# Fused attention, soft mixture of experts and gated FFN: the heads in another order, a load later, the weight conversion two steps ahead, and the copies of a step behind the next silu

## The chip, the core and the metric

The kernel runs on one core of one Trainium2 chip. The metric is the device time of one execution in microseconds (us). The core's engines are TensorE (PE, with its weight loads as PEld), VectorE (DVE), ScalarE (ACT), GpSimd (POOL) and SyncE (SP); 16 DMA engines move data between HBM and the on-chip memory. Each engine takes its instructions in the order in which the program gives them to it, and waits on semaphores for the others.

## The reference

Three stages follow each other; everything is float32 except the FFN weights, which arrive as float64.

```python
# q, k, v: 4 batches x 8 heads x 576 x 64
scores = q @ k.T / 8                      # heads 0..3: local mask, 0 <= i-j < 32
                                          # heads 4..7: strided mask, i >= j and i%32 == j%32
x = softmax(mask(scores)) @ v             # heads side by side: x is 2304 x 512

logits = x @ phi                          # 32 slots = 8 experts x 4
d = softmax(logits over the 2304 tokens)
slot = d.T @ x                            # 32 x 512
slot_out[e] = relu(slot[e] @ w1[e]) @ w2[e]       # w1: 8 x 512 x 1024, w2: 8 x 1024 x 512
x = softmax(logits over the 32 slots) @ slot_out  # c @ slot_out, 2304 x 512

g = x @ w_gate                            # 512 x 1536
out = (g * sigmoid(g) * (x @ w_val)) @ w_out      # 1536 x 512, out is 2304 x 512
```

## The kernel before

**Attention (0 to 117 us).** A unit is one head of two batches (a batch pair); there are 16, in the order of `HORDER`, each in three steps t of three blocks of 64 query rows. The tokens of the strided heads are laid out so that their mask is a narrow band too, which makes both kinds of head the same work with widths 96 and 80. The loop takes two steps at a time, n and n+1: the score matmuls (`qk`, L296) of both, DVE's mask and maximum (L302), ACT's exponential (L314), the transposes of the step two before (`tr`, L321) with ACT's copy of them (L324), the product with v of the step four before (`pv`, L334), and DVE's normalisation. Behind the second head of each pair of heads the rows are transposed (`xtr`, L360) and multiplied with phi (`logits`, L380, 8 matmuls; a strided pair writes its tokens back in the plain order). Once all four pairs of heads of a batch pair have added to one bank of PSUM, `tok_max` and the token softmax follow.

**Loads.** SP issues the loads in program order: q, k and v of a unit some units ahead (L267, L268, L274), and between them halves of 1 MB weight tiles (`load_half`, L178). These go into 14 buffers called `w`, into the three shared tiles `s1`, `s0`, `s2`, which also hold q, k, v and the local mask `ml`, and into attention's own tiles. Eight semaphores are used in turn for the loads, so that each load waits until the one eight before it has landed. `WORDER` gives the order in which the weights take the 14 buffers; a later load into the same buffer waits for the last reader of the earlier one.

**Mixture of experts (117 to 153 us).** 16 weight tiles w1 (`w1_mm`, L656) and 16 tiles w2 (L745) are used as they land. Between the matmuls of w2, `c_soft` makes the softmax over the slots (two halves) and eight `c_tr` turn it (3 transposes each, L716, and a DVE copy, L719) into `cs`; the table `CTR` tells after which w2 tile.

**FFN (153 to 360 us).** Since x = c @ slot_out, the kernel first multiplies the weights by slot_out. For each of 12 column tiles f, `a_mm` (L805) makes soT x w, ACT copies it (`asb`, L808), `a_st` (L812) spreads it and ACT and DVE split it into `St` (L813, L814). The FFN then runs over a list of steps (a range of f by five token blocks): `gv` (two matmuls, L825 and L826), silu on ACT (`sg`, L831), the product on DVE (`h`, L832), its high part on ACT (`hh`, L833) and the rest of it on POOL (`hl`, L834). `omm` (12 matmuls, L852) of a step runs `LAG` = 3 steps behind it. `h` has two buffers, so that h of a step waits for hl of the step two before; hh and hl have four. The partial sums go to `acc` by ACT or DVE (L875) or are added to it by DVE (L878), and the last range writes `out` (L880, L861).

**Weight conversion.** The float64 weights arrive as pairs of words. Tiles g (gate and value of one f) and o (two rows of f of the last matrix) are converted in halves: ACT takes the magnitude (L227, the first half of `prep`), POOL clamps it (L228), and DVE does three parts, `shift`, `low`, `sign` (L232, L236, L240), in the order of `ORDER`. `stage` starts a half on ACT and POOL, `part` runs one DVE part; at most two halves are staged, and parts are run in a step as far as its room goes. `force` does what is missing at once when a step needs a tile that isn't ready: all instructions that stand before it, `a_mm` and `a_st` too. `HEAD` is the order at the entry of the FFN: a = a_mm, s = a_st, g = stage, w = a warm matmul, p = parts. `load_g` (L686) loads the FFN's weights into four `g` tiles, which are laid over the memory of the `w` tiles and the first of which waits for whatever last used it.

Of the kernel before, what the change touches and what calls it, by code (L numbers as in the profile page):

```python
# [17 lines left out]
S = 576  # L18
# [6 lines left out]
HORDER = (0, 1, 4, 5, 2, 3, 6, 7)  # L25
# [7 lines left out]
WORDER = list(range(1, 13)) + list(W2ORDER[:2])  # L33
# [5 lines left out]
LAG = 3  # L39
WT = (0, 0)  # L40
# [3 lines left out]
CTR = {9: 1, 10: 1, 11: 1, 12: 1, 13: 1}  # L44
CTE = (1,)
SLOT0 = [(4, [(0, 0, 9)]), (6, [(1, 0, 5)]), (8, [(1, 5, 9)])]
STG = 1
# [8 lines left out]
HEAD = "a0 a1 g s0 w1 s1 p1 w1"  # L56
# [55 lines left out]
def build(ctx: ExitStack, tc: tile.TileContext, cst, phi, qh, kh, vh, w1, w2, wgv, wo, out):  # L112
# [34 lines left out]
    ml, ms = s1[:, VW + K:VW + K + 192], s3[:, VW + S:VW + S + 720]  # L147
# [158 lines left out]
    def expo(u, t):  # L306
        W = WID[UNITS[u][1] // 4]
        sm, mx = sc.pop((u, t))
        o = 288 * ((3 * u + t) % 2)
        e = tmp[:, o:288 + o].rearrange("p (j k) -> p j k", j=3)  # L310
        if W < 96 and u % 4 == 2 and t < 2:
            DVE.memset(e[:, :, 0:96 - W], 0.0)
        for j in range(3):
            ACT.activation(out=e[:, j, 96 - W:96], in_=sm[:, j, 0:W], func=AF.Exp, scale=-1.0, bias=mx[:, j:j + 1])  # L314
        ex[u, t] = e
# [50 lines left out]
    def logits(bp, y, st):  # L366
        first, last = (y, st) == (0, 0), (y, st) == (1, 1)
        if first:
            lg[bp] = bank("lg", 1)
        a = xT.pop((bp, y, st))  # L370
        for hf in range(2):
# [145 lines left out]
    with tc.manual_schedule():  # L517
# [16 lines left out]
        load_half(2)  # L534
# [40 lines left out]
        for bp in range(2):  # L575
            for y in range(2):
                for st in range(2):
                    u = 8 * bp + 4 * st + 2 * y + 1
# [134 lines left out]
        def c_tr(bp, b, hf):  # L713
            ps = bank("tr", 2)
# [6 lines left out]
        ctr = [(c_tr, (bp, b, hf)) for bp in range(2) for b in range(2) for hf in range(2)]  # L721
# [20 lines left out]
        for n, j in enumerate(W2ORDER):  # L742
# [7 lines left out]
            if n < 2:  # L750
                c_soft(n)
# [3 lines left out]
            for _ in range(CTR.get(n, 0)):  # L755
                fn, a = ctr.pop(0)
                fn(*a)
# [63 lines left out]
        def gv(bi, f):  # L821
# [11 lines left out]
            ACT.copy(hh[bi, f][:, 0:n], h[:, 0:n])  # L833
            POOL.tensor_tensor(out=hl[bi, f][:, 0:n], in0=h[:, 0:n], in1=hh[bi, f][:, 0:n].bitcast(F32),  # L834
                               op=ALU.subtract)
# [4 lines left out]
        def omm(p, bi, f):  # L840
# [6 lines left out]
            def mm(t, terms):  # L847
                z = len(ob[t])
                c = 512 // z
                for k, o in enumerate(ob[t]):  # L850
# [4 lines left out]
                    if last and 2 in terms:  # L855
                        if end:
# [4 lines left out]
                            SP.dma_start(out=out[r:r + 128, c * k:c * k + c], in_=tmp[:, 0:c])  # L861
# [70 lines left out]
        split_hi(0)  # L932
        split_lo(0, 0)
        split_lo(0, 1)
        for step in HEAD.split():
# [5 lines left out]
            elif k == "g":  # L941
                stage(-2)
            elif k == "p":
# [4 lines left out]
        for n in range(len(seq) + LAG):  # L948
# [17 lines left out]
            if n < len(seq):  # L966
                force(n, ("g", seq[n][2]))
                gv(*seq[n][1:])
            while staged and staged[0][0] <= n and PART <= room:
                room -= PART  # L970
                part(n)
            if n >= STG:
                stage(n)
                if n < 2 * STG:
                    stage(n)
# [20 lines left out]
```

## Time and profile before

| What | Value |
|---|---|
| Time, median of 3 runs (lowest to highest) | 361.76 us (359.48 to 364.25) |
| Profiled execution: its time, its span | 362.2 us, 360.4 us |
| Mean granted TensorE clock | 0.994 |
| PE busy | 338.7 us, 94% |
| PEld busy | 243.9 us, 68% |
| DVE busy | 219.4 us, 61% |
| ACT busy | 186.8 us, 52% |
| POOL busy | 132.6 us, 37% |
| DMA moved | 71.94 MB, mean 200 GB/s |

The profile is of one execution on the hardware. Busy times overlap between engines; a share over the whole span is a mean over stages with different limits. The span of the profiled execution starts at its first instruction, and its time is 1.8 us longer than that.

### The profile page before, as it was taken

Reading aid. Unit: us, or ns where it says so; the run is one execution under the profiler, and the core shown is the slowest. Engines: PE = TensorE matmul, PEld = TensorE weight load, DVE = VectorE, ACT = ScalarE, POOL = GpSimd, SP = SyncE. Lnnn points to the kernel's source line nnn. Section 1 sums busy time; section 2 is a strip of 40 time slices with the busy share of each in tenths; the row PEclk is TensorE's granted clock in tenths of the full one; section 3 lists DMA queues with packets and bytes.
Section 4 is the critical chain, followed back from the end, with each engine's and each line's share of the span. In section 5 each row is a group of like instructions: output and inputs, shape, how many; then the busy total and the mean of one; then the engine's idle time right before and its main releaser. Section 6 shows DMA issues by size and latency. Waiting matters only on the chain.

```text
span 360.4 us, 7681 instructions
## 1 busy us (share of the span) xinstructions
PE 338.7 (94%) x2856; PEld 243.9 (68%) x2856; DVE 219.4 (61%) x707; ACT 186.8 (52%) x449; POOL 132.6 (37%) x163
## 2 busy tenths in 40 slices
PE   7799989899989999978999899999998999999995
PEld 4677766787737443345777487777785787878774
DVE  4868785765546017247877788788859844142432
ACT  3877969766842003256666565465535653434321
POOL 1522323122110020036555475485525774434431
PEclk9999999999999999998999999999999999999999
DMA  7998998959998999684232542154300003030304
GB/s 212 398 400 299 348 369 322 303 201 352 341 411 303 367 409 408 254 333 172 85 127 102 161 160 73 74 198 154 116 0 2 2 2 116 0 115 4 117 30 144
DMA packets 23397, 71.94 MB, mean 200 GB/s; under 512 B 2624, under 2 KB 3520, under 8 KB 23360
## 3 DMA queue, kind: packets, MB, share of 16 engines
q1 hardware_dynamic: 23216, 71.45, 53.9%
q8 instruction: 22, 0.36, 0.4%
q14 instruction: 15, 0.12, 0.1%
q10 hardware_dynamic: 144, 0.01, 0.0%
HBM read 66.73 MB, written 4.72 MB: 198 GB/s over the span
## 4 chain that ended last, share of the span: by engine, by line
PE 75%; DMA 8%; DVE 6%; ACT 5%; issue 3%; SPq 2%; POOL 1%; DVEq 0%; ACTq 0%
PE o L852 38%; PE sc L296 5%; PE pv L334 5%; PE pv L745 4%; PE gv L825 4%; PE tr L321 3%; DMA w<-in_w 3%; PE gv L826 3%; PE tr L360 2%; PE lg L380 2%; DMA s<-in_kh 2%; PE ms L445 2%; DMA s<-in_qh 2%; DMA g<-in_wgv 1%; DVE h L832 1%
## 5 line engine op out<-in xcount | busy, mean ns | idle before, releaser
L834 POOL TENSOR_TENSOR hl<-h,hh 128x512 fp32r<-128x512 f32 (+1 forms) x60 | 71.0, 1183 | 90.7 <-ACT hh L833 90.7
L852 PE MATMUL o<-woh,hh 128*128 128x512 f32 (+1 forms) x220 | 88.2, 401 | 3.1 <-ACT acc L875 1.7
L852 PE MATMUL o<-wol,hh 128*128 128x512 f32 (+1 forms) x220 | 85.6, 390 | 0.0
L832 DVE TENSOR_TENSOR h<-gv,sg 128x512 f32<-128x512 f32 (+1 forms) x59 | 37.5, 635 | 49.8 <-ACT sg L831 40.0
L833 ACT CAST hh<-h 128x512 fp32r<-128x512 f32 (+1 forms) x60 | 34.7, 578 | 55.3 <-DVE h L832 55.3
L852 PE MATMUL o<-woh,hl 128*128 128x512 f32 (+1 forms) x220 | 59.3, 386 | 0.0
L852 PEld LDWEIGHTS o<-woh,hh 128*128 128x128 f32 x220 | 41.7, 190 | 17.8 <-DVE acc L878 3.1
L277 POOL COPY s<-s 32x390 f32<-32x390 f32 (+1 forms) x48 | 23.8, 498 | 68.4 <-DMA s<-in_vh 46.9
L831 ACT ACTIVATE sg<-gv 128x512 f32<-128x512 f32 (+1 forms) x60 | 33.4, 556 | 26.3 <-PE gv L825 26.2
L852 PEld LDWEIGHTS o<-wol,hh 128*128 128x128 f32 x220 | 41.8, 190 | 7.6
L852 PEld LDWEIGHTS o<-woh,hl 128*128 128x128 f32 x220 | 41.1, 188 | 8.6
L314 ACT ACTIVATE tmp<-tmp,mx 128x96 f32<-128x96 f32 (+1 forms) x144 | 40.8, 363 | 3.0 <-DVE mx L302 3.0
L302 DVE CUSTOM_DVE_ANT_0 tmp<-sc,s 128x96 f32<-128x96 f32 (+1 forms) x144 | 28.1, 245 | 17.6 <-PE sc L296 16.4
L296 PEld LDWEIGHTS sc<-s,s 64*64 64x64 f32 x576 | 23.1, 132 | 13.1 <-issue 7.5
L296 PE MATMUL sc<-s,s 64*64 64x96 f32 (+1 forms) x576 | 27.8, 240 | 4.5 <-DMA s<-in_kh 1.7
L324 ACT COPY tmp<-tr 96x384 f32<-96x384 f32 x47 | 20.2, 477 | 20.6 <-PE tr L321 20.5
L825 PE MATMUL gv<-cs,St 128*128 128x512 f32 (+1 forms) x60 | 25.4, 423 | 2.4 <-DVE St L814 2.4
L796 POOL TENSOR_TENSOR wol<-wo,woh 128x512 fp32r<-128x512 f32 x12 | 15.5, 1297 | 24.0 <-ACT woh L793 24.0
L334 PE MATMUL pv<-s,tmp 96*64 96x65 f32 x576 | 22.4, 225 | 0.6 <-POOL s L277 0.6
L826 PE MATMUL gv<-cs,St 128*128 128x512 f32 (+1 forms) x59 | 22.6, 383 | 0.2 <-DVE h L832 0.2
L334 PEld LDWEIGHTS pv<-s,tmp 96*64 96x64 f32 x576 | 19.0, 137 | 4.0 <-issue 0.8
L321 PE MATMUL tr<-cst_t,tmp 128*96 128x128 f32 x144 | 21.1, 280 | 0.4 <-ACT xT L361 0.4
(164 smaller groups left out, 456.6 us busy)
## 6 DMA issues: line engine op xcount, KB each, us to landing
w<-in_w SPq DMA_DIRECT2D x50, 512.0 KB, 8.4
g<-in_wgv SPq DMA_DIRECT2D x10, 1024.0 KB, 5.1
g<-in_wo SPq DMA_DIRECT2D x5, 1024.0 KB, 4.9
s<-in_vh SPq DMA_DIRECT2D x16, 292.5 KB, 6.1
out<-osb SPq DMA_DIRECT2D x17, 256.0 KB, 2.2
s<-in_qh SPq DMA_DIRECT2D x15, 288.0 KB, 6.2
s<-in_kh SPq DMA_DIRECT2D x15, 288.0 KB, 6.3
wx<-in_w SPq DMA_DIRECT2D x7, 512.0 KB, 5.1
```

The source lines that it names most:

```text
L296: PE.matmul(out=ps[r, W * j:W * j + W], lhsT=qt[u % AHEAD][r, 64 * i:64 * i + 64], rhs=kt[u % AHEAD][r, c0:c0 + W], start=True, stop=True, ...
L302: DVE.tensor_tensor_reduce(out=sm[:, j, 0:W], in0=ps[:, W * j:W * j + W], in1=mask(y, 3 * t + j), scale=-0.125, scalar=3.0e38, op0=ALU.add ...
L314: ACT.activation(out=e[:, j, 96 - W:96], in_=sm[:, j, 0:W], func=AF.Exp, scale=-1.0, bias=mx[:, j:j + 1])
L321: PE.transpose(ps[0:96, 128 * j:128 * j + 128], e[:, j, :], ident)
L334: PE.matmul(out=ps[64 * b:64 * b + 64, o:o + 65], lhsT=a[:, j, 64 * b:64 * b + 64], rhs=vt[u % AHEAD][:, 65 * (NT * b + 3 * t + j):65 * (N ...
L825: PE.matmul(out=pg[:, 0:n], lhsT=St[f][:, 0:128], rhs=csf[:, t0:t0 + n], start=True, stop=True)
L826: PE.matmul(out=pvv[:, 0:n], lhsT=St[f][:, 128:256], rhs=csf[:, t0:t0 + n], start=True, stop=True)
L831: ACT.activation(out=sg[:, 0:n], in_=pg[:, 0:n], func=AF.Silu)
L832: DVE.tensor_tensor(out=h[:, 0:n], in0=pvv[:, 0:n], in1=sg[:, 0:n], op=ALU.mult)
L833: ACT.copy(hh[bi, f][:, 0:n], h[:, 0:n])
L834: POOL.tensor_tensor(out=hl[bi, f][:, 0:n], in0=h[:, 0:n], in1=hh[bi, f][:, 0:n].bitcast(F32), op=ALU.subtract)
L852: PE.matmul(out=o[:, 0:c], lhsT=(a, a, l)[i][:, 128 * t:128 * t + 128], rhs=(woh, wol, woh)[i][f][:, c * k:c * k + c], start=(first and i ...
```

## The change

Eight edits, in the order of the program:

- `HORDER`: in each batch pair the units come as local, local, strided, strided, strided, strided, local, local; before, the last four were local, local, strided, strided. `logits`, its `last` flag and the step at which it runs follow.
- The local mask `ml` moves from the shared tile s1 to s0.
- The first half tiles of FFN weights (g 0, two loads) are no longer issued in front of q and k of unit 3, but behind them.
- `WORDER`: weight tiles 12 and 11 swap buffers.
- Both halves of `c_soft` stand after the second w2 tile, and the eight `c_tr` stand 3 after tile 10, 3 after tile 14 and 2 behind the last; before, 5 were after tiles 9 to 13.
- `HEAD` stages half a g tile before the first `a_mm` and takes two of its DVE parts before the first `a_st`; at step 1 (`STG`) only one half is staged.
- `AHEAD_H` = 12: for steps below 12, hh and hl of a step are issued behind silu and h of the next step.
- The last output transfer is issued by ACT's queue, not by SP's.

```diff
-HORDER = (0, 1, 4, 5, 2, 3, 6, 7)
+HORDER = (0, 1, 4, 5, 6, 7, 2, 3)
...
-WORDER = list(range(1, 13)) + list(W2ORDER[:2])
+WORDER = list(range(1, 11)) + [12, 11] + list(W2ORDER[:2])
...
+AHEAD_H = 12
...
-CTR = {9: 1, 10: 1, 11: 1, 12: 1, 13: 1}
+CTR = {10: 3, 14: 3}
...
-HEAD = "a0 a1 g s0 w1 s1 p1 w1"
+HEAD = "h g l a0 a1 p2 s0 w1 s1 g p1 w1"
...
-    ml, ms = s1[:, VW + K:VW + K + 192], s3[:, VW + S:VW + S + 720]
+    ml, ms = s0[:, K + 2 * S:K + 2 * S + 192], s3[:, VW + S:VW + S + 720]
...
-        if W < 96 and u % 4 == 2 and t < 2:
+        if W < 96 and u % 8 == 2 and t < 2:
             DVE.memset(e[:, :, 0:96 - W], 0.0)
...
-    def logits(bp, y, st):
-        first, last = (y, st) == (0, 0), (y, st) == (1, 1)
+    def logits(bp, y, st, halves=(0, 1)):
+        first, last = (y, st) == (0, 0), (y, st) == (0, 1)
...
         load_v(1)
         load_v(2)
-        load_half(2)
...
-                    u = 8 * bp + 4 * st + 2 * y + 1
+                    u = 8 * bp + 4 * st + 2 * (y != st) + 1
...
-        ctr = [(c_tr, (bp, b, hf)) for bp in range(2) for b in range(2) for hf in range(2)]
+        ctr = [(c_tr, (bp, b, hf)) for hf in range(2) for bp in range(2) for b in range(2)]
...
             if n == HID1:
                 hid(1)
-            if n < 2:
-                c_soft(n)
+                c_soft(0)
+                c_soft(1)
...
-            for _ in range(CTR.get(n, 0)):
+            for k in range(CTR.get(n, 0)):
                 fn, a = ctr.pop(0)
-                fn(*a)
+                fn(*a, bk=("lg", 1) if k == 2 else ("tr", 2))
...
-            ACT.copy(hh[bi, f][:, 0:n], h[:, 0:n])
-            POOL.tensor_tensor(out=hl[bi, f][:, 0:n], in0=h[:, 0:n], in1=hh[bi, f][:, 0:n].bitcast(F32),
-                               op=ALU.subtract)
+            split_h()
+            hs_.append((h[:, 0:n], hh[bi, f][:, 0:n], hl[bi, f][:, 0:n]))
+
+        hs_ = []
+
+        def split_h():
+            while hs_:
+                h, a, l = hs_.pop()
+                ACT.copy(a, h)
+                POOL.tensor_tensor(out=l, in0=h, in1=a.bitcast(F32), op=ALU.subtract)
...
-                            SP.dma_start(out=out[r:r + 128, c * k:c * k + c], in_=tmp[:, 0:c])
+                            (ACT if t and k else SP).dma_start(out=out[r:r + 128, c * k:c * k + c], in_=tmp[:, 0:c])
...
-        split_hi(0)
-        split_lo(0, 0)
-        split_lo(0, 1)
         for step in HEAD.split():
...
+            elif k == "h":
+                split_hi(0)
+            elif k == "l":
+                split_lo(0, 0)
+                split_lo(0, 1)
...
                 gv(*seq[n][1:])
+                if n >= AHEAD_H:
+                    split_h()
...
             if n >= STG:
                 stage(n)
-                if n < 2 * STG:
-                    stage(n)
```

SP's queue behind the loads of v of units 1 and 2, before (`in_qh`, `in_kh`, `in_vh` are q, k and v; the number of a tile is its buffer):

```order
L274 DMA s_78<-in_vh 64x1170
L274 DMA s_80<-in_vh 64x1170
L178 DMA w<-in_wgv 128x1024 x2
L267 DMA s_81<-in_qh 128x576
L268 DMA s_79<-in_kh 128x576
L178 DMA w<-in_wgv 128x1024 x2
```

The same place in the changed kernel:

```order
L275 DMA s_78<-in_vh 64x1170
L275 DMA s_80<-in_vh 64x1170
L268 DMA s_81<-in_qh 128x576
L269 DMA s_79<-in_kh 128x576
L179 DMA w<-in_wgv 128x1024 x2
L275 DMA s_81<-in_vh 64x1170
```

The two loads of q and k of unit 3 have moved past two loads of 512 KB.

SP's queue at the end of the weights and the first FFN load, with the semaphores that each waits for, before (DMAHW0 to DMAHW7 are the eight semaphores of the loads; the last two `w` loads carry DMAHW0 and DMAHW1):

```order
L178 DMA w<-in_w 128x1024 [waits DMAHW0_49,PE_49]
L178 DMA w<-in_w 128x1024 [waits DMAHW1_49]
L686 DMA g<-in_wgv 128x2x1024 [waits DMAHW0_49,DMAHW1_49,DVE_49,DMAHW2_49,PE_49,Pool_49]
L686 DMA g<-in_wgv 128x2x1024 [waits DMAHW7_49,DMAHW6_49,DMAHW3_49]
L686 DMA g<-in_wo 128x2x1024 [waits DMAHW4_49]
```

The same place in the changed kernel:

```order
L179 DMA w<-in_w 128x1024 [waits DMAHW0_49,PE_49]
L179 DMA w<-in_w 128x1024 [waits DMAHW1_49]
L686 DMA g<-in_wgv 128x2x1024 [waits DVE_49,DMAHW2_49,PE_49,Pool_49]
L686 DMA g<-in_wgv 128x2x1024 [waits DMAHW6_49,DMAHW7_49,DMAHW3_49,PE_49]
L686 DMA g<-in_wo 128x2x1024 [waits DMAHW4_49]
```

The first FFN load no longer waits for the landing of the last two `w` loads. Its PE wait was for the matmul of the last w2 tile (L745) and is now for the last w1 tile's (L656); the second load's, new, is for the w2 tile before the last.

ACT's queue at the entry of the FFN, before:

```order
L793 CAST woh_2356<-wo_60 128x512
L793 CAST woh_2357<-wo_60 128x512
L808 COPY asb<-gv 128x256
L808 COPY asb<-o 128x256
L227 ACTIVATE wg_2333<-g 128x512
L813 CAST St_2344<-gv 128x256
L813 CAST St_2345<-o 128x256
L831 ACTIVATE sg<-gv 128x512
L833 CAST hh<-h 128x512
L831 ACTIVATE sg<-gv 128x512
L833 CAST hh<-h 128x512
```

The same place in the changed kernel:

```order
L793 CAST woh_2352<-wo_60 128x512
L793 CAST woh_2353<-wo_60 128x512
L228 ACTIVATE wg_2329<-g 128x512
L808 COPY asb<-gv 128x256
L808 COPY asb<-o 128x256
L813 CAST St_2340<-gv 128x256
L813 CAST St_2341<-o 128x256
L228 ACTIVATE wg_2329<-g 128x512
L831 ACTIVATE sg<-gv 128x512 x2
L841 CAST hh<-h 128x512
```

The magnitude of the first g half has moved past both copies `asb`, and the first `hh` past the second silu.

## Rows read from the trace of the kernel before

**Rows 1.** The page: span, and the chain that ended last by engine.

```profile
span 360.4 us, 7681 instructions
...
PE 75%; DMA 8%; DVE 6%; ACT 5%; issue 3%; SPq 2%; POOL 1%; DVEq 0%; ACTq 0%
```

**Rows 2.** Stretches: us, PE, PEld, DVE, ACT, POOL busy, clock, DMA, GB/s.

```profile
110.00:117.00 7.00, 6.93 (x91) 5.66 (x90) 4.04 (x16) 1.79 (x6) 0.00 (x0) 1.00 0.79 275
133.00:150.00 17.00, 16.91 (x141) 6.03 (x141) 8.78 (x26) 5.22 (x8) 0.00 (x0) 1.00 1.00 397
150.00:168.00 18.00, 14.76 (x79) 8.01 (x77) 8.20 (x16) 9.05 (x19) 7.65 (x8) 0.91 0.63 240
280.00:320.00 40.00, 40.00 (x180) 31.83 (x179) 17.99 (x28) 18.77 (x33) 21.77 (x18) 1.00 0.07 27
```

**Rows 3.** The chain, 8 to 19 us: start, us, what.

```profile
10.48 7.33 DMA s<-in_kh
```

**Rows 4.** ACT's timeline, 15.8 to 21 us: start, us, instructions, idle before.

```profile
17.76 1.21 ACT L197 ACTIVATE wg<-w 128x512 f32<-128x512 f32 x2
20.04 0.85 ACT L324 COPY tmp<-tr 96x384 f32<-96x384 f32 x2 [1.07 <-PE tr L321]
```

**Rows 5.** PE's timeline in attention, five places.

```profile
18.05 0.63 PE L296 MATMUL sc<-s,s 64*64 64x80 f32 x12 [1.71 <-DMA s<-in_kh]
...
51.24 0.71 PE L296 MATMUL sc<-s,s 64*64 64x96 f32 x12 [1.16 <-DVE wg L211]
...
58.53 1.26 PE L380 MATMUL lg<-xT,phi_t 128*32 128x288 f32 x8
...
97.65 0.69 PE L380 MATMUL lg<-xT,phi_t 128*32 128x288 f32 x8
...
104.49 1.26 PE L380 MATMUL lg<-xT,phi_t 128*32 128x288 f32 x8 [0.57 <-ACT xT L361]
```

**Rows 6.** SP's timeline, 100 to 155 us: weight loads, first FFN loads.

```profile
118.90 23.51 SPq L178 DMA_DIRECT2D w<-in_w  x22
153.12 0.90 SPq L686 DMA_DIRECT2D g<-in_wgv  x2
```

**Rows 7.** DMA issues, 141.7 to 142.3 us, the last weight load: us to landing.

```profile
w<-in_w SPq DMA_DIRECT2D x1, 512.0 KB, 10.2
```

**Rows 8.** ACT's timeline, 153 to 160 us.

```profile
153.62 1.15 ACT L793 CAST woh<-wo 128x512 fp32r<-128x512 f32 x2
...
158.27 0.66 ACT L227 ACTIVATE wg<-g 128x512 f32<-128x512 f32 x1 [1.41 <-DMA g<-in_wgv]
...
159.08 0.38 ACT L813 CAST St<-o 128x256 fp32r<-128x256 f32 x1
```

**Rows 9.** PE's timeline, 153 to 171 us.

```profile
159.70 0.50 PE L825 MATMUL gv<-cs,St 128*128 128x512 f32 x1 [1.79 <-DVE St L814]
...
163.29 0.63 PE L852 MATMUL o<-woh,hh 128*128 128x512 f32 x1
...
168.23 0.50 PE L852 MATMUL o<-woh,hh 128*128 128x512 f32 x1 [1.36 <-ACT acc L875]
```

**Rows 10.** DVE's timeline, 153 to 171 us.

```profile
168.46 1.28 DVE L875 COPY acc<-o 128x512 f32<-128x512 f32 x2
```

**Rows 11.** PE's timeline, three later places.

```profile
204.38 0.63 PE L805 MATMUL gv<-wg,soT 128*32 128x256 f32 x4 [0.51 <-DVE wg L240]
205.64 0.50 PE L825 MATMUL gv<-cs,St 128*128 128x512 f32 x1 [0.63 <-DVE St L814]
...
278.59 0.50 PE L852 MATMUL o<-woh,hh 128*128 128x512 f32 x1 [1.27 <-DVE acc L878]
```

**Rows 12.** SP's timeline at the end.

```profile
356.52 1.30 SPq L861 DMA_DIRECT2D out<-osb  x3
```

**Rows 13.** POOL's timeline, 167 to 169 us.

```profile
167.22 1.28 POOL L834 TENSOR_TENSOR hl<-h,hh 128x512 fp32r<-128x512 f32 x1 [0.59 <-ACT hh L833]
168.47 0.61 POOL L228 TENSOR_SCALAR wg<-wg 128x512 f32<-128x512 f32 x1
```

More of the change, by code (lines that the diff above doesn't have):

```diff
@@ L364, in build @@
     lg = {}
-    def logits(bp, y, st):
-        first, last = (y, st) == (0, 0), (y, st) == (1, 1)
+    def logits(bp, y, st, halves=(0, 1)):
+        first, last = (y, st) == (0, 0), (y, st) == (0, 1)
         if first:
             lg[bp] = bank("lg", 1)
-        a = xT.pop((bp, y, st))
-        for hf in range(2):
+        a = xT[bp, y, st]
+        for hf in halves:
             for b in range(2):
@@ L711, in c_soft, with c_tr @@
             ACT.copy(t4[:, :, 2:4, :], t4[:, :, 0:2, :].bitcast(F32))
-        def c_tr(bp, b, hf):
-            ps = bank("tr", 2)
+        def c_tr(bp, b, hf, bk=("tr", 2)):
+            ps = bank(*bk)
             for k in range(3):
```

## The prediction

> **What bounds the kernel now.** I read the page first. The span is 360.4 us, and three quarters of the chain that ended last are PE's [rows 1]. So a change counts only where PE waits, or where PE gets less to do. The table by stretch then tells the stages apart [rows 2]. From 280 to 320 us PE is busy for all of its 40 us: nothing can be had there except fewer matmuls, and the change removes none. From 133 to 150 us PE looks full too, but the DMA share is 1.00 at 397 GB/s: the stage of w2 is paced by its weights. From 150 to 168 us, the entry of the FFN, PE is busy for 14.76 of 18 us and its granted clock is 0.91: here is the largest loss that isn't work. The timelines of single engines then show each wait, by its start and by the bracket that names what ended it.
>
> **The start.** PE stands idle for 1.71 us before the scores of unit 3 at 18.05, released by its k [rows 5]. That load was issued at 10.48 and took 7.33 us, so it landed at 17.81 [rows 3]. The change takes two loads of 512 KB out from in front of q and k of unit 3; at 397 GB/s [rows 2] that is 1.05 MB / 397 GB/s = 2.6 us. So k lands at about 15.2 and PE's 1.71 us go. What is late next is ACT: it runs two magnitudes from 17.76 to 18.97 and then waits 1.07 us, until 20.04, for PE's transposes [rows 4]. The magnitudes stay where they are in ACT's order, and the copy can't start before them. Of the 1.71 us only 1.07 are gained, 0 and 1.71 being the ends. The moved loads now run beside later ones; the wait at 51.24 (1.16 us, [rows 5]) sits in that later stream, and it is why 0 is an end.
>
> **The heads.** Logits of a strided pair take 1.26 us, of a local pair 0.69 [rows 5]: 0.57 apart. The pairs that end with units 5 and 13 become strided, those that end with 7 and 15 local. Unit 5's extra 0.57 falls just ahead of the idle 1.16 at 51.24 and is covered by it (if that wait went, it would cost 0.57). Unit 7's saving at 58.53 is on PE's path: 0.57. Unit 13's extra falls at 97.65 on a PE that then waits 0.57 at 104.49 for ACT's copy; unit 15's saving is at 104.49, straight on the way to the token softmax. I take 0.3 for the two together, between 0 and 0.57.
>
> Start and heads are 1.07 + 0.57 + 0.3 = 1.9 us at the end of attention. They reach the FFN only if the weights come earlier too, since w2 ends with its last landing. From 110 to 117 us the DMA share is 0.79 [rows 2], so 0.21 x 7 = 1.5 us of the DMA engines are free; behind that they are full, and no byte is saved. **I take 1.5**, with ends at -0.6 (unit 5's and 13's extra uncovered, nothing from the start, 0.57 back) and 2.2.
>
> **The entry of the FFN.** Before, the first FFN load is issued at 153.12 [rows 6], because it waits for the last w2 tile's landing and matmul; ACT's first magnitude waits 1.41 us for it and starts at 158.27; the copies of St stand behind it in ACT's order, to 159.08 + 0.38 [rows 8]; and PE waits 1.79 us, until 159.70, for St [rows 9]. In the change this load waits only for w1's last matmul and early landings, so it may be issued while the last of the 22 weight loads are on their way: the last of these is issued at about 142 (118.90 + 23.51 less its own issue, [rows 6]) and takes 10.2 us [rows 7], so it lands at about 152. The DMA engines go on with 1.05 MB at 397 GB/s, 2.6 us: landed at 154.6. ACT is busy with woh until 153.62 + 1.15 = 154.77 [rows 8], so the magnitude, now ahead of `asb`, finds its data there and runs in the time in which ACT would wait for `a_mm`. The copies of St start as their matmuls end. Two DVE parts now stand ahead of the DVE half of St, so not all of the 1.79 goes: I take 1.6.
>
> The next wait is 1.36 us at 168.23, for ACT's copy of `acc` [rows 9], which stands behind a magnitude (0.66 us) and hh; DVE's two copies, from 168.46 for 1.28 [rows 10], stand behind three conversion parts. In the change one magnitude and two parts are done earlier, before gv starts. I take 1.0 of the 1.36. **Together 2.6**; the ends are 0 and 1.79 + 1.36 = 3.2, plus what the clock gives (below).
>
> **The conversion, later.** At 204.38 and 205.64 PE waits 0.51 and 0.63 us for the last DVE part of a weight tile and for its St [rows 11]: the tile was needed before its parts had had their turn, and `force` ran them all at once. With the conversion two parts ahead nothing is forced there. **1.1 us**, between 0 and all of it, 1.14. At 278.59 PE waits 1.27 us for DVE's sum into `acc` [rows 11]; two parts fewer stand in DVE's order then. **I take 0.5**, between 0 and 1.27.
>
> **The end.** Three output transfers are issued by SP within 1.30 us [rows 12], 0.43 each. The last, from ACT's idle queue, needs no turn behind the second: **0.4**, between 0 and 0.43.
>
> **Costed at nothing.** The eight `c_tr` hold the same transposes; six instead of five stand before the last w2 tile, where PE waits for weights anyway; uncovered, one set of three transposes moves. The mask's tile only frees s1 earlier for a weight load whose queue is full. hh and hl behind the next silu: silu comes earlier by one hh, hl later by about one step, and `omm` runs three steps behind; the slow rival below is its price.
>
> **The sum** is 1.5 + 2.6 + 1.1 + 0.5 + 0.4 = 6.1 us. Against the profiled execution (362.2 us, the span and 1.8 around it) it gives 356.1; that execution is 0.4 above the median of 361.76, against which it gives 355.7. I forecast **356.0**, its own range 353.5 to 358.5.
>
> **Rivals.**
>
> *More than the sum* (353.4). PE's matmuls at 163.29 take 0.63 us, at 168.23 0.50: the first run at the lower of the two clock levels (1.2 and 2.4 GHz), after the thin stretch in which PE waits 1.79 us [rows 9], and a granted clock of 0.91 over 18 us [rows 2] is 0.09 x 18 = 1.6 us. If the shorter wait keeps the clock at its upper level, this comes on top, with the rest of the waits at 168.23 (0.36) and 278.59 (0.77): 2.7 us, 356.1 - 2.7 = 353.4. Against it: while DVE paces the first steps, a quicker PE only waits. The Trainium skill's page "TensorE: Matmul & The Clock Gate" (section "HAM oscillation — how this bites in real kernels") has PE fall to half rate when waits for data come between its bursts; the row at 163.29 agrees, and by it this rival would hold. Chance 0.20.
>
> *The first load comes late* (359.7). The magnitude of g 0 now stands in ACT's order ahead of both `asb`. If the load lands where it landed before, less the 1.5 us of attention (158.2 - 1.5 = 156.7), then asb, its matmul, the copy of St and DVE's half follow the magnitude one after another instead of being done: 0.66 and five steps of about 0.38 (the copy's length, [rows 8]) are 2.6, so gv starts at 159.3 instead of 159.70 - 1.5 = 158.2. The 2.6 are lost and 1.0 more: 6.1 - 3.6 = 2.5 gained, 359.7. It decides as soon as the load lands later than about 155.5. For it: eight loads must have landed before the next is issued, and the DMA engines are full. Against it: what this load waits for is done by about 143. The Trainium skill's page "TensorE: Matmul & The Clock Gate" (section "Architectural detail: the array is 16× 32×32, not 1× 128×128") calls ACT's queue a strict FIFO, which speaks against this edit: whatever stands behind a late magnitude is late too, as the copies of St behind it at 158.27 show. Chance 0.14.
>
> *Attention gives nothing* (357.6). The wait at 18.05 returns elsewhere in the load stream, or the last weights land when they did. 6.1 - 1.5 = 4.6. For it: DMA shares of 1.00. Chance 0.11.
>
> *Slower than before* (363.7). In the first twelve steps hl(n-2) is issued only behind silu(n-1), and h(n) needs its buffer back. From silu's end: hh (as long as a magnitude, 0.66), a clamp on POOL ahead (0.61) and hl (1.28) [rows 8, 13] make 2.55 us. A step is 14 matmuls; 180 in 40 us [rows 2] make 3.1 us. So 0.55 are spare. Where POOL has one more subtract (1.28) ahead, h is 0.7 late; if that happens in all of eleven steps and reaches PE, 11 x 0.7 = 7.7 us are lost, 356.0 + 7.7 = 363.7. Against it: only the o tiles bring such a subtract, and `omm` has three steps of slack. Chance 0.05.
>
> **Numbers.** Forecast 0.50, and the rivals 0.20, 0.14, 0.11 and 0.05. The range for 8 in 10 runs from 351.9 (every term at its better end and the clock: 2.2 + 3.2 + 1.6 + 1.1 + 1.3 + 0.4 = 9.8 below the median) to 360.3 (0.6 above the late first load). Two per cent is about what a measurement of this kernel can tell from no change: below 354.5 or above 369.0. Faster takes most of the first rival and a third of the forecast's own range: 0.35. Slower by that much needs the last rival and more: 0.02. The rest, 0.63, is within 2%.
>
> **What would show it.** PE's wait before the scores of unit 3 shrinks to below 0.7 us, and ACT's copy stands right behind the magnitudes. The first g load is issued before the last w load has landed and lands near 155 less attention's gain; ACT shows no wait for it; PE's wait before the first gv falls below 0.5. Behind the first steps no PE wait names L240 or L814 near 203 us. The last two output transfers start on two queues within 0.2 us. I am wrong if POOL's hl becomes the releaser of h in most early steps, if ACT waits for g 0 ahead of asb, or if the last w load lands no earlier than 151.9.

## The result, and the profile after

The changed kernel takes 358.19 us (median of 20 runs, 355.56 to 360.36), the kernel before 361.38 us in its 20. The ratio is 0.9913 with a 95% interval of 0.9891 to 0.9935: 3.2 us faster, and clearly so, though less than 2%. The profiled execution took 357.49 us, 4.7 us less than that of before. Three runs behind the table of experiments below (one of ahead0, one of b_start, one of the kernel before in the second group) were in a slower state; the ratios leave them out, the medians and clocks there don't.

The page of the changed kernel, which answers to [rows 1]:

```profile
span 355.7 us, 7689 instructions
...
PE 76%; DVE 10%; ACT 8%; issue 3%; DMA 1%; POOL 1%; DVEq 0%; ACTq 0%; POOLq 0%
```

The span is 4.7 us shorter, and DMA's share of the chain has gone from 8% to 1%. The table by stretch, with the columns of [rows 2], and three stretches of the start:

```profile
4.00:13.00 9.00, 7.33 (x92) 5.70 (x92) 5.65 (x44) 4.13 (x14) 2.41 (x6) 0.81 0.96 330
13.00:27.00 14.00, 13.01 (x254) 10.71 (x249) 11.80 (x78) 11.79 (x38) 4.27 (x8) 1.00 0.84 300
27.00:37.00 10.00, 8.04 (x128) 6.26 (x131) 7.76 (x38) 6.55 (x21) 3.48 (x6) 1.00 1.03 403
110.00:117.00 7.00, 6.93 (x93) 5.52 (x90) 3.99 (x17) 2.02 (x7) 0.00 (x0) 1.00 0.84 290
133.00:150.00 17.00, 16.67 (x143) 6.81 (x143) 8.21 (x25) 5.22 (x8) 0.00 (x0) 1.00 1.03 408
150.00:168.00 18.00, 16.36 (x96) 9.61 (x94) 14.25 (x26) 10.81 (x22) 9.28 (x10) 1.00 0.78 298
280.00:320.00 40.00, 40.00 (x174) 31.86 (x173) 16.18 (x25) 16.29 (x28) 19.17 (x16) 1.00 0.15 53
```

From 150 to 168 us PE is busy for 16.36 us in place of 14.76, and the granted clock is 1.00 in place of 0.91. From 280 on nothing has changed. But the start shows something new: a clock of 0.81 from 4 to 13 us, and a DMA share of 0.84 from 13 to 27 us. In the kernel before, the clock was 1.00 in both stretches, and the share in the second was 1.03:

```profile
13.00:27.00 14.00, 12.05 (x229) 9.82 (x227) 10.37 (x69) 11.66 (x37) 5.30 (x11) 1.00 1.03 403
```

The low clock from 4 to 13 us belongs to this one execution: in the traces of old_worder, old_head, ahead0 and b_start (below), which issue the same loads up to there, it is 1.00. The lower DMA share is in all of them, at 0.91 to 0.98.

PE's timeline of the changed kernel, before unit 5 (to be held against [rows 5]):

```profile
30.06 0.63 PE L297 MATMUL sc<-s,s 64*64 64x80 f32 x12 [1.73 <-DVE mx L303]
```

PE's timeline at the entry of the FFN, which answers to [rows 9]:

```profile
157.72 0.50 PE L825 MATMUL gv<-cs,St 128*128 128x512 f32 x1 [0.29 <-DVE St L814]
...
160.28 0.50 PE L859 MATMUL o<-woh,hh 128*128 128x512 f32 x1 [0.39 <-ACT hh L841]
...
163.58 0.39 PE L859 MATMUL o<-woh,hh 128*128 128x512 f32 x1
...
165.40 0.50 PE L859 MATMUL o<-woh,hh 128*128 128x512 f32 x1 [0.75 <-DVE acc L882]
```

PE's timeline at two later places, which answer to [rows 11]:

```profile
211.74 0.50 PE L859 MATMUL o<-woh,hh 128*128 128x512 f32 x1 [0.81 <-DVE acc L885]
...
274.63 0.49 PE L859 MATMUL o<-woh,hh 128*128 128x512 f32 x1 [0.55 <-DVE acc L885]
```

The first gv waits 0.29 us instead of 1.79 and the second omm isn't stopped at its first matmul any more. The two waits near 203 us are gone; one of 0.81 has come at 211.74, and that of 1.27 has shrunk to 0.55. Before unit 5, where there was no wait, stands one of 1.73; the bracket names DVE, but k of unit 5 landed at 29.92, just ahead of the start at 30.06.

How far each milestone of PE moved, read off the starts of the same matmuls in the two traces (us, a minus is earlier):

| Milestone | Before | After | Moved |
|---|---|---|---|
| Scores of unit 3 (second half of a step pair) | 18.05 | 17.35 | -0.70 |
| Scores of unit 5 | 28.41 | 30.06 | +1.65 |
| Last score of attention's last pair of steps | 94.55 | 94.91 | +0.36 |
| Last w2 tile's last matmul | 152.45 | 152.15 | -0.30 |
| First gv | 159.70 | 157.72 | -1.98 |
| Second omm | 168.23 | 163.58 | -4.65 |
| Third omm | 172.52 | 168.73 | -3.79 |
| Omm's 133rd matmul of 660 (behind the forced tile) | 207.61 | 201.91 | -5.70 |
| Omm's 349th matmul | 271.90 | 268.22 | -3.68 |
| Last matmul | 356.19 | 351.56 | -4.63 |

So in these two executions attention gave 0.3 us, the entry of the FFN 3.5 (from -0.30 to -3.79), what follows 0.8 net, the end nothing.

The first row of the table is too small, because the low clock at the start stands in front of it: old_worder, old_head and ahead0, with the same attention, have these scores at 15.77, 15.57 and 16.26, while b_worder and b_wo_ah, with the attention of before, have them at 17.36 and 17.38.

### The profile page after: what moved, and what is told of

Same layout as the page of the kernel before. It is cut to its first block, busy times and chain, and to the rows that moved or that the text cites. A ratio compares the mean times of both kernels' runs of the same rounds, so it can differ in the third digit from the quotient of the medians.

```text
span 355.7 us, 7689 instructions
## 1 busy us (share of the span) xinstructions
PE 338.4 (95%) x2856; PEld 245.2 (69%) x2856; DVE 219.3 (62%) x703; ACT 185.9 (52%) x449; POOL 132.2 (37%) x163
## 4 chain that ended last, share of the span: by engine, by line
PE 76%; DVE 10%; ACT 8%; issue 3%; DMA 1%; POOL 1%; DVEq 0%; ACTq 0%; POOLq 0%
PE o L859 35%; PE sc L297 6%; PE pv L335 5%; PE tr L322 4%; PE sc L656 4%; PE pv L745 4%; PE gv L825 3%; PE gv L826 3%; PE tr L361 2%; PE lg L381 2%; PE ms L446 2%; DVE h L832 2%; ACT tmp L325 1%; DMA g<-in_wgv 1%; ACT tmp L315 1%
## 5 line engine op out<-in xcount | busy, mean ns | idle before, releaser
L297 PEld LDWEIGHTS sc<-s,s 64*64 64x64 f32 x576 | 24.2, 137 | 12.2 <-issue 5.6
L297 PE MATMUL sc<-s,s 64*64 64x96 f32 (+1 forms) x576 | 28.7, 246 | 3.4 <-DVE mx L303 3.4
L229 POOL TENSOR_SCALAR wg<-wg 128x512 f32<-128x512 f32 x20 | 12.3, 617 | 28.1 <-DMA g<-in_wgv 24.4
```

The costliest lines, as they stand in the source:

```text
L297: PE.matmul(out=ps[r, W * j:W * j + W], lhsT=qt[u % AHEAD][r, 64 * i:64 * i + 64], rhs=kt[u % AHEAD][r, c0:c0 + W], start=True, stop=True, ...
```

## The experiments

All were timed beside the kernel before, whose medians in the three groups were 361.21, 361.54 and 361.23 us. "Clock" is the mean over a kernel's runs of the granted clock that each run lists; over 63 runs of the kernel before it was 0.994.

| Kernel | Median us (runs) | Ratio, 95% interval | Clock | Last w2 | First gv | Second omm | Last matmul |
|---|---|---|---|---|---|---|---|
| before | 361.38 (20) | 1 | 0.994 | 152.45 | 159.70 | 168.23 | 356.19 |
| changed | 358.19 (20) | 0.9913 [0.9891, 0.9935] | 0.995 | 152.15 | 157.72 | 163.58 | 351.56 |
| no_att | 356.21 (6) | 0.9871 [0.9831, 0.9912] | 0.997 | 150.94 | 156.52 | 162.41 | 350.35 |
| old_worder | 361.68 (12) | 1.0002 [0.9972, 1.0032] | 0.989 | 153.19 | 162.08 | 168.25 | 356.16 |
| old_head | 357.52 (6) | 0.9898 [0.9862, 0.9934] | 0.998 | 152.48 | 157.87 | 163.92 | 352.81 |
| ahead0 | 358.89 (12) | 0.9935 [0.9903, 0.9967] | 0.994 | 150.08 | 155.64 | 163.60 | 352.24 |
| b_worder | 361.34 (12) | 1.0000 [0.9969, 1.0031] | 0.992 | 151.94 | 157.69 | 166.20 | 355.73 |
| early_load | 357.00 (6) | 0.9890 [0.9861, 0.9918] | 0.995 | 151.72 | 157.28 | 163.18 | 351.05 |
| b_start | 363.00 (12) | 1.0039 [1.0005, 1.0073] | 0.991 | 152.48 | 159.41 | 167.92 | 357.39 |
| fill4 | 355.08 (5) | 0.9838 [0.9810, 0.9867] | 1.000 | 149.22 | 154.79 | 160.69 | 348.54 |
| b_wo_ah | 357.33 (12) | 0.9896 [0.9866, 0.9925] | 0.998 | 151.81 | 157.58 | 163.46 | 352.23 |
| fill4_oldh | 355.37 (6) | 0.9835 [0.9801, 0.9869] | 1.000 | 150.31 | 155.88 | 161.77 | 349.66 |

The last four columns are of one execution each. Where the work up to w1 is the same, its end still scatters: the first w1 matmul starts at 117.61 in the changed kernel, at 117.81 in old_head and at 115.11 in ahead0, whose attention is the same. Single traces therefore say where a wait is; how much attention is worth is said by the medians. What lies between the last w2 and the last matmul repeats much better: 199.3 to 199.4 us in the changed kernel, no_att, early_load, fill4 and fill4_oldh.

### What does attention give, and what does the entry need?

**no_att**: the attention edits undone.

```diff
-HORDER = (0, 1, 4, 5, 6, 7, 2, 3)
+HORDER = (0, 1, 4, 5, 2, 3, 6, 7)
...
         load_v(2)
+        load_half(2)
```

> The changed kernel with its attention edits undone (HORDER with its logits, the tile of the local mask, the place of the first weight load); everything from w1 on as in the change. Theory (attention gave nothing, as the trace after shows with 0.3 us at the last w2 tile): 358.2 us, ratio to before 0.991, within 0.4% of the changed kernel; PE reaches the last w2 tile within 0.3 us of the changed kernel. Rival (the 1.5 us that I took for attention are there, and the profiled execution hid them): 359.7 us, ratio 0.995, and the last w2 tile 1.5 us later.

It ran at 356.21 us, 2 us below the changed kernel. Neither of my theories had this: the attention edits don't give nothing, they cost. The intervals of the two ratios still touch (0.9912 and 0.9891), so the size is loose.

**old_worder**: the swap of two buffers undone.

```diff
-WORDER = list(range(1, 11)) + [12, 11] + list(W2ORDER[:2])
+WORDER = list(range(1, 13)) + list(W2ORDER[:2])
```

> The changed kernel with the old WORDER alone, so that the first FFN load again waits for the last w2 tile, while its magnitude stands ahead of asb in ACT's order. Theory (ACT's order makes a late load hold up asb too): the first gv starts near 160.5, 2.8 us later than in the changed kernel (157.7), and 361 to 362 us. Rival (only the load's own lead is lost, asb doesn't matter): the first gv near 159.4, 359.9 us.

It ran at 361.68 us: the first theory holds, and without the swap the whole gain is gone (the attention edits, which cost, are still in this kernel). ACT's and PE's timelines of this kernel show how:

```profile
158.75 0.66 ACT L228 ACTIVATE wg<-g 128x512 f32<-128x512 f32 x1 [3.24 <-issue]
159.31 0.36 ACT L808 COPY asb<-gv 128x256 f32<-128x256 f32 x1
159.56 0.38 ACT L808 COPY asb<-o 128x256 f32<-128x256 f32 x1
```

PE's, in the same stretch:

```profile
159.72 0.90 PE L812 MATMUL gv<-asb,cst_t 128*128 128x256 f32 x2 [2.92 <-ACT asb L808]
```

ACT waits 3.24 us and starts the magnitude at 158.75; the trace names no releaser ("issue"), but the load that it reads is issued at 153.85 in this kernel, behind the last w2 matmul as in the kernel before, and lands at 158.68. Both `asb` copies, whose matmuls had long been done, stand behind it, and PE waits 2.92 us for them. The first gv starts at 162.08, later than before (159.70) and later than the 160.5 that I had written.

**old_head** and **ahead0** undo the other two parts of the entry. The first:

```diff
-HEAD = "h g l a0 a1 p2 s0 w1 s1 g p1 w1"
+HEAD = "a0 a1 g s0 w1 s1 p1 w1"
...
                 stage(n)
+                if n < 2 * STG:
+                    stage(n)
```

> The changed kernel with the old HEAD and the second stage at step 1 back: the load stays early, but no half tile is converted ahead. Theory (the conversion ahead is worth what the trace shows between the 10th and 12th omm, 2.3 us, part of it given back later): 359.5 us, PE waits of 0.5 us and more for L240 and L814 near 202 us again, first gv 0.3 to 0.6 us later. Rival (all of the forced stall is given back later, or the early load alone carries it): 358.2 us.

The second:

```diff
-AHEAD_H = 12
+AHEAD_H = 0
```

> The changed kernel with AHEAD_H = 0: hh and hl directly behind h in all steps. Theory of the prediction (the delay costs nothing and brings nothing): 358.2 us. Rival 1 (a silu in front of hh is what lets the second omm start 2.7 us earlier beyond the entry): 360 us, the second omm 1 us later or more. Rival 2 (the delay keeps h waiting for POOL): 356.5 us.

old_head ran at 357.52 us: not slower than the changed kernel, the rival's side. Its PE waits again 0.51 us for L241 and 0.63 for L814, at 200.85 and 202.11, as in [rows 11], and yet from the first gv to the last matmul it needs only 194.94 us, 1.1 more than the changed kernel's 193.84; the medians can't tell that apart. Its first gv, at 157.87, is 0.15 us later than the changed kernel's, less than I had written.

ahead0 ran at 358.89 us, and its median can't be told from the changed kernel's either; rival 1's 360 us did not come. But its trace shows the mechanism of rival 1: from the first gv to the last matmul it needs 196.60 us, 2.8 more. PE's timeline of this kernel at the second omm:

```profile
163.60 0.69 PE L859 MATMUL o<-woh,hh 128*128 128x512 f32 x1 [1.87 <-ACT acc L882]
164.09 0.63 PE L859 MATMUL o<-wol,hh 128*128 128x512 f32 x1
164.51 0.63 PE L859 MATMUL o<-woh,hh 128*128 128x512 f32 x1
```

With hh in front of the second silu the wait for ACT's `acc`, which I had written off, is 1.87 us, and behind it the matmuls start 0.42 us apart instead of 0.23: the lower of the two clock levels (1.2 and 2.4 GHz). The wait follows from the order on ACT; the low clock behind it is not in every execution, since seven of this kernel's twelve runs list 0.998 or 0.999 and the traced one 0.993.

**b_worder** and **b_wo_ah** put the parts on the kernel before, one and then two: the swap of WORDER alone, and with it the change's `split_h` and AHEAD_H = 12.

```diff
-WORDER = list(range(1, 13)) + list(W2ORDER[:2])
+WORDER = list(range(1, 11)) + [12, 11] + list(W2ORDER[:2])
```

b_wo_ah has this line, and:

```diff
+AHEAD_H = 12
...
-            ACT.copy(hh[bi, f][:, 0:n], h[:, 0:n])
-            POOL.tensor_tensor(out=hl[bi, f][:, 0:n], in0=h[:, 0:n], in1=hh[bi, f][:, 0:n].bitcast(F32),
-                               op=ALU.subtract)
+            split_h()
+            hs_.append((h[:, 0:n], hh[bi, f][:, 0:n], hl[bi, f][:, 0:n]))
```

> The kernel before with the WORDER swap alone. Theory (the early first load is the largest single step, and it needs the rest only in part): the first g load issued near 143 and landed near 154.5, PE's wait before the first gv gone, first gv near 158.1, 1.6 us earlier; but hh still stands in front of the second silu, so the second omm gains no more than that; 359.5 to 360 us, ratio 0.995. Rival (the swap alone carries the whole gain): 358 us, ratio 0.991. Rival 2 (nothing without the conversion ahead): 361.4.

> The kernel before with the WORDER swap and AHEAD_H = 12, nothing else (old HEAD, old CTR, attention as before). Theory (the entry has two waits in series, for the first load and for ACT's copies of acc, and either one left open lets the clock drop; these two edits close both): 357.5 us, ratio 0.989, no drop of the clock between 150 and 172 us, the second omm 4 us or more earlier than before, the forced stall near 203 us still there. Rival (HEAD's early magnitude is needed too): 360 us or more, ratio above 0.995, with the clock lower at the second omm as in the kernel with the swap alone.

b_worder ran at 361.34 us, the second rival's number, though its first load is as early as I had said. Its PE timeline:

```profile
157.69 0.50 PE L825 MATMUL gv<-cs,St 128*128 128x512 f32 x1 [0.29 <-DVE St L814]
...
166.20 0.50 PE L852 MATMUL o<-woh,hh 128*128 128x512 f32 x1 [1.98 <-ACT acc L875]
...
167.51 0.63 PE L852 MATMUL o<-woh,hh 128*128 128x512 f32 x1
```

And its stretch from 150 to 172 us, with the columns of [rows 2]:

```profile
150.00:172.00 22.00, 19.03 (x100) 10.94 (x100) 12.59 (x22) 11.90 (x25) 10.61 (x11) 0.92 0.64 234
```

The first gv is at 157.69, 2.0 us earlier than before; the wait of 1.36 at 168.23 [rows 9] has become 1.98. ACT's timeline of this kernel shows what sets it:

```profile
159.59 0.62 ACT L833 CAST hh<-h 128x512 fp32r<-128x512 f32 x1 [0.76 <-DVE h L832]
...
161.46 0.62 ACT L833 CAST hh<-h 128x512 fp32r<-128x512 f32 x1 [0.76 <-DVE h L832]
```

ACT stands still for DVE's h before each hh, and the next silu and the copy of `acc` stand behind it in its order. The second omm follows the first gv by 8.51 us here and by 8.53 in the kernel before, although PE ran the first omm at the upper clock here and at the lower one there (the row at 163.29). So in the trace of before, the low clock at the first omm cost nothing: PE would only have waited longer for ACT.

In this kernel the lower clock comes behind the second omm's wait (0.63 in place of 0.40 per matmul), where it does cost: at the third omm only 0.6 us of the 2.0 are left (171.92 against 172.52). The mean clock from 150 to 172 us is 0.92 in both kernels. That the swap moved the low clock is not shown. b_start (below), whose entry is that of the kernel before, has it behind the second omm too:

```profile
159.41 0.50 PE L824 MATMUL gv<-cs,St 128*128 128x512 f32 x1 [1.46 <-DVE St L813]
...
167.92 0.50 PE L851 MATMUL o<-woh,hh 128*128 128x512 f32 x1 [1.96 <-ACT acc L874]
...
169.06 0.63 PE L851 MATMUL o<-woh,hh 128*128 128x512 f32 x1
```

b_wo_ah ran at 357.33 us, and its clock from 150 to 168 us is 1.00:

```profile
150.00:168.00 18.00, 16.34 (x93) 9.02 (x89) 11.64 (x21) 10.58 (x22) 9.30 (x10) 1.00 0.68 247
```

PE's timeline of it at the forced tile:

```profile
200.45 0.62 PE L806 MATMUL gv<-wg,soT 128*32 128x256 f32 x4 [0.50 <-DVE wg L241]
201.71 0.50 PE L826 MATMUL gv<-cs,St 128*128 128x512 f32 x1 [0.63 <-DVE St L815]
```

These two edits carry 3.9 us, as much as the whole change. In this kernel, and in the seven others with the delay, the second omm follows the first gv by 5.86 to 6.17 us. The clock is the smaller part of the 3.9: among the runs that list 0.999 or more, the kernel before has a median of 360.6 us (12 runs) and b_wo_ah 357.3 (6 runs), which leaves 3.3 us with the clock up in both.

The swap without the delay gave nothing (b_worder), and the delay without the swap gave nothing either, though only with HEAD's early magnitude and the attention edits beside it (old_worder); the delay alone was not run. With the rest of the change beside it, the swap without the delay gave 2.3 us (ahead0, 358.89), so there something in the rest does part of what the delay does. HEAD and the new places of `c_tr` are the candidates; no run separates them, and `CTR` was not run alone. The first two stalls of [rows 11] are still there in b_wo_ah.

### Where does the start's gain go?

**b_start**: the kernel before, with the first weight loads behind q and k of unit 3, and nothing else.

```diff
         load_v(1)
         load_v(2)
-        load_half(2)
```

> The kernel before with the first two weight loads moved behind q and k of unit 3, and nothing else. Theory: PE's wait of 1.7 us before unit 3 goes, a wait of 1 to 3 us comes before unit 5, in some executions with a lower clock behind it: 361.4 to 363 us, ratio 1.000 to 1.005. Rival (it gives its 1.1 us, the heads' order loses them): 360.3 us, ratio 0.997.

It ran at 363.00 us, slower than the kernel before by an interval that excludes 1. PE's timeline of this kernel:

```profile
28.36 0.73 PE L296 MATMUL sc<-s,s 64*64 64x96 f32 x12 [2.43 <-DMA s<-in_kh]
29.02 1.57 PE L334 MATMUL pv<-s,tmp 96*64 96x65 f32 x24
```

The stretch behind it, with the columns of [rows 2]:

```profile
27.00:37.00 10.00, 8.64 (x113) 6.66 (x113) 5.57 (x30) 5.09 (x16) 4.09 (x8) 0.83 1.03 400
```

The wait before unit 3 is gone, and PE is 2.65 us ahead of before at 25 us; then it waits 2.43 us for k of unit 5. The 24 products with v behind that wait take 1.57 us in place of 0.92, and the clock of the stretch is 0.83. Unit 5 needs the same bytes ahead of its k as before, wherever the two weight loads stand among them: k landed at 28.22 here and at 27.36 before. The start can run ahead only as far as the loads do, and the wait that ends it cost more than it had won. In old_worder and old_head, with the same start, the wait before unit 5 is 2.25 and 2.94 us and the clock from 27 to 37 us 0.83 as well; in the changed kernel and in ahead0 it is 1.73 and 1.14 us, and the clock stays at 1.00.

**early_load** and **fill4** try two other places for these loads in the changed kernel: in front of q and k of unit 3 as before, and behind them but all four halves at once.

```diff
         load_v(2)
+        load_half(2)
```

> The changed kernel with the first two weight loads back in front of q and k of unit 3; HORDER and the mask's tile stay changed. Theory (those two loads keep the DMA engines busy while SP waits for v's buffer, and taking them away costs the start's gain again before unit 5): PE waits 1.7 us before unit 3 and nothing, or below 0.5 us, before unit 5; DMA share from 13 to 27 us at 1.0 again; no drop of the clock from 27 to 37 us; 356.3 us, as the kernel without the attention edits, ratio 0.987. Rival (the order of the heads is what costs): 358 us, ratio 0.991.

```diff
                 load_qk(3)
-                load_half(2)
+                load_half(4)
```

> The changed kernel with all four halves of the first two weight tiles right behind q and k of unit 3, ahead of v of unit 3, instead of two of them. Theory (filler is what was missing): k of unit 3 still lands near 14, the DMA engines stay busy during SP's wait for v's buffer, k of unit 5 lands before 27.5, no wait above 0.5 us before units 3 and 5; 355.5 us, ratio 0.984, below the kernel without the attention edits. Rival (the wait only moves on to another unit): 357 to 358 us, ratio 0.990.

early_load ran at 357.00 us, between the two numbers, with waits of 0.69 us before unit 3, less than the 1.7 that I had written, and 0.66 before unit 5, more than my 0.5. Its DMA share from 13 to 27 us is 1.02, as the theory had it. It has the new order of heads and no_att the old one; their medians, 0.8 us apart, can't be told apart. fill4 ran at 355.08 us, the fastest of all, 3.1 us below the changed kernel with intervals apart. Its stretch from 13 to 27 us:

```profile
13.00:27.00 14.00, 12.56 (x237) 10.16 (x233) 11.57 (x75) 12.23 (x41) 5.12 (x11) 1.00 1.03 406
```

PE's timeline before unit 5:

```profile
27.05 0.63 PE L297 MATMUL sc<-s,s 64*64 64x80 f32 x12 [0.52 <-DVE wg L208]
```

The difference to the changed kernel is one line of SP's queue. There, only two halves are issued behind k of unit 3, SP then waits until 15.91 for the buffer of v of unit 3, and the next two halves stand behind v, q and k. The DMA engines run partly dry (a share of 0.84 from 13 to 27 us, above), and k of unit 5 lands at 29.92. With four halves on the way during that wait the share is 1.03, k of unit 5 lands at 26.92, and PE waits 0.52. SP's wait is longer than usual in the changed kernel's trace, whose start ran at the low clock. But the difference is there without that: in old_worder, old_head, ahead0 and b_start SP's wait ends at 13.26 to 14.33, the share is 0.91 to 0.98 and k of unit 5 lands at 27.62 to 28.87; in fill4_oldh (below) the share is 1.01 and k lands at 27.44.

**fill4_oldh** is fill4 with the old order of heads and the old tile of the mask.

```diff
-HORDER = (0, 1, 4, 5, 6, 7, 2, 3)
+HORDER = (0, 1, 4, 5, 2, 3, 6, 7)
...
-                load_half(2)
+                load_half(4)
```

> The kernel with all four halves behind q and k of unit 3, with the old order of heads and the mask's old tile. Theory (the order of heads gives the 0.6 to 0.9 us that I put on it, once no wait for a load hides it): 355.8 us, ratio 0.986, the last w2 tile 0.6 to 0.9 us later than with the new order. Rival (the order of heads is worth nothing): 355.1 us, ratio 0.984. Rival 2 (it costs): 354.5 us.

It ran at 355.37 us, which the medians can't tell from fill4's 355.08. In the traces fill4's last w2 matmul is 1.09 us earlier, but executions of one program differ by more than that. Whether the order of heads is worth 0.3 us, nothing, or costs a little (early_load against no_att) stays open.

## Why the prediction was right, and where it wasn't

The time lay in the range and the sign was right; 356.0 was 2.2 us too low. That it came so near is in part luck: one term turned into a loss, and another was larger than forecast. By its terms:

- **Start and heads: 1.5 predicted, 0.3 in the trace, and a loss by the medians.** This is the step that failed. The gain at unit 3 came, 0.70 us in this execution and more in others. The cap of 1.07, by ACT's magnitudes at 17.76, did not hold: with an earlier PE ACT is earlier too (in b_start its magnitudes start at 16.28), and b_start is 2.65 us ahead at 25 us. But the moved loads were not free: the bytes in front of unit 5's k stayed, and SP's wait for v's buffer now found too little on the way. I had named the place of the risk (the loads that run beside later ones), and priced it at its end of "nothing". The chance 0.11 for "attention gives nothing" (357.6) was too low; that rival was nearest to the median. What I hadn't thought of is a loss: b_start shows +1.4 us (1.0039) for this edit alone, with the clock in it. Of the 0.9 for the heads, fill4 against fill4_oldh shows 0.3 at most, which can't be told from nothing. The last w load landed at 151.64, only 0.3 us ahead of the 151.9 that I had named as a sign of being wrong. The upper end of 2.2 was too low by the term's own numbers, since it takes 1.07 for the start where the text gives 1.71 as its end.
- **The entry: 2.6 predicted, 3.5 measured.** The first part, 1.6 until the first gv, was right: 1.7 from the last w2 (-0.30 to -1.98). The early load is issued at 142.77 and lands at 154.20, where I had put 154.6. SP's timeline, which answers to [rows 6]:

```profile
119.14 22.63 SPq L179 DMA_DIRECT2D w<-in_w  x22
142.77 7.83 SPq L686 DMA_DIRECT2D g<-in_wgv  x2
```

  ACT's timeline, which answers to [rows 8], has no wait for it:

```profile
154.36 0.68 ACT L228 ACTIVATE wg<-g 128x512 f32<-128x512 f32 x1
155.44 0.37 ACT L808 COPY asb<-gv 128x256 f32<-128x256 f32 x1 [0.40 <-PE gv L805]
...
157.25 0.37 ACT L813 CAST St<-o 128x256 fp32r<-128x256 f32 x1 [0.28 <-PE o L812]
...
158.25 1.09 ACT L831 ACTIVATE sg<-gv 128x512 f32<-128x512 f32 x2
159.61 0.62 ACT L841 CAST hh<-h 128x512 fp32r<-128x512 f32 x1 [0.27 <-DVE h L832]
```

  The second part, 1.0, was 1.8 by the third omm. I had put the gain there on DVE's parts and one magnitude; b_worder against b_wo_ah (4.0 us by the medians) shows that it comes with the two silus back to back (158.25 x2), which I had costed at nothing. ACT then waits 0.27 us before the first hh, in place of 0.76 before each of two, and its copy of `acc` comes earlier. DVE's copies [rows 10] were not what the second omm waited for, though part of the gain is given back at a wait of 0.75 us for DVE's `acc` at 165.40.
- **The conversion: 1.1 + 0.5 predicted, 1.1 to 1.3 measured.** The forced stall went as forecast, and gave 2.3 us between omm's 121st and 133rd matmul (-3.42 to -5.70). By the 349th most of that was given back, to -3.68, in part in the new wait at 211.74 for DVE's sum into `acc`. The wait of 1.27 at 278.59 lost 0.72, and with what stands around it that makes 1.06 by the 397th matmul (-3.68 to -4.74). From the 121st on this is 1.3 us; old_head puts the whole of HEAD at 1.1. The sum is near, its two terms are not.
- **The end: 0.4 predicted, nothing measured.** From the last matmul's start to the last landing both kernels need 3.1 us, and so do all the others (3.11 to 3.15). The issue is earlier, but the transfer from ACT's queue took 2.2 us where SP's last had taken 1.9. SP's timeline, which answers to [rows 12]:

```profile
351.88 0.81 SPq L868 DMA_DIRECT2D out<-osb  x2
```

  ACT's timeline:

```profile
352.55 0.35 ACTq L868 DMA_DIRECT2D out<-osb  x1
```

  And its DMA issue, whose last number is the us from issue to landing:

```profile
out<-osb ACTq DMA_DIRECT2D x1, 128.0 KB, 2.2
```

- **The rivals.** *More than the sum* saw rightly that the clock at the entry would stay up (1.00 in place of 0.91), but its 1.6 us were not there to be had in the trace that it was read from: the second omm waited for ACT, with or without the low clock in front of it, as the prediction's own objection said. Among the runs that list a clock of 0.999 or more, the kernel before has a median of 360.6 us (12 runs) and the changed one 356.4 (3 runs): there the gain is 4.2 us, and hardly any of it is the clock's. *The first load comes late* didn't come, since the swap frees the load; old_worder shows that its mechanism is as described, with 2.92 us at the place named, and that 359.7 was too kind (its 361.68 has the loss in attention in it). *Slower than before* didn't come: in the changed kernel's trace POOL's hl releases h only once, at 287.94, against seven times before, and moving hh was a gain.

The gains of the entry and the loss at the start are shown by kernels that hold one of them alone. That the lower clock follows from the waits in front of it is only suggested by the rows: no run here set the clock by itself, and waits of like length stand without it (1.71 us before unit 3 in the kernel before, 1.73 before unit 5 in the changed one, both with a clock of 1.00 behind them).

## What to carry to other kernels

Two waits in a row can hide each other's price: with the first taken away, PE stood longer at the second (1.98 us in place of 1.36), and in that trace a spell of the lower clock behind it cost more of the rest. Try the edits in pairs before dropping one that measured nothing. Before pricing a stretch at the lower clock, look whether the next wait would have eaten the time anyway. A load that is moved out of the way of an urgent one needs a place where the queue's next stall still finds enough on the way. And before an instruction is put ahead of others on an in-order engine, look up what its data waits for: the same order went without a wait with an early load, and cost a wait of 2.92 us with a late one.

## What the runs showed of the hardware

The spread of this kernel's times goes with the granted clock that each run lists: of the kernel before, runs at 0.999 and more had a median of 360.6 us against 361.3 over all 63. All five runs of fill4 had 0.998 or more and lay within 1.1 us; those of the changed kernel went from 0.988 to 1.000 and lay within 4.8 us. It isn't the whole of it: early_load's six runs lay within 1.0 us, four of them at 0.993. I had not expected that kernels with fewer waits would spread less. The place of the low clock differs between traces with the same attention and nearly the same rest: 0.81 from 4 to 13 us in the changed kernel, 0.83 from 27 to 37 us in old_head, 0.66 from 163 to 168 us in ahead0. One trace can so hold a spell that the next doesn't. The last output transfer gained nothing from a second queue: issued 0.67 us behind the first instead of 0.90, it took 0.3 us longer.
